# A fused attention and mixture-of-experts kernel: constants, weight casts and the interleaving of a batch's steps with the FFN are reordered

## The chip, the cores and the metric

The kernel runs on one core of a Trainium2 chip. The metric is the device time of one execution in microseconds (us). A comparison of two kernels is always made on one chip, in rounds that run both; the time of the kernel before differs between chips by up to 1.4% (medians from 247.9 to 251.3 us in this study), so ratios are compared across calls, and absolute times only within one. All runs quoted here are in what the record calls the fast state: none is over 1.5% above the fastest of its kernel in the same rounds.

The engines are named as the profile names them: PE is TensorE (matmuls), PEld its weight loads, DVE is VectorE, ACT is ScalarE, POOL is GpSimd, SP is SyncE.

## The reference

```python
# q, k, v: (batch 8, heads 8, seq 576, head_dim 64), fp32
def _attn_ref(q, k, v):
    q_s = exp(q - max over dims);  q_s /= sum over dims + 1e-9
    k_s = exp(k - max over seq);   k_s /= sum over seq + 1e-9
    kv = np.einsum('bhsd,bhse->bhde', k_s, v)
    return np.einsum('bhsd,bhde->bhse', q_s, kv)

# x: the 4608 tokens of 512 elements; 8 experts of 1024 hidden elements
def _moe_ref(x, modality_id, w_gate, modality_bias, w1, w2):
    logits = x @ w_gate + modality_bias[modality_id]
    e_idx = np.argmax(logits, axis=1)
    gate_w = softmax(logits)[token, e_idx]
    for e in range(E):
        mask = e_idx == e
        h = np.maximum(x[mask] @ w1[e], 0.0)
        out[mask] = gate_w[mask, None] * (h @ w2[e])
```

(Shortened: the two softmaxes and the token reshaping are written in one line each.)

## The kernel before

The kernel loads two experts: the one that each modality's bias row favours. (A loop at the end redoes tokens that chose another; it is not entered here.) It goes through the eight batches in order. For each, `prep` exponentiates k and q on ScalarE and casts v; `attend` multiplies k with v (`kv_ps`), scales the result into `kvbd`, turns q and kv (`tp_ps`, `kvT_ps`), and gets the logits (`g_ps`, `lg_ps`); `route` decides the expert of each token, counts places (`r_ps`), and moves the tokens, sorted, into `xs` (`xT_ps`). Each is a generator. `weave` runs a batch's steps and, at every `yield x`, adds `x * rate` to what is owed in FFN pieces of earlier batches. A piece is some 0.9 us of matmuls (0.86 us from the one at 75.81 us in batch 2 to what follows it); it keeps PE busy while the other engines work on the batch.

```python
def prep(b, v_eng):                      # six steps: k, k, v, v, q, q
    ...
            for nm in "kvq":
                ...                      # v: copy_on(v_eng, vb, st);  k, q: ACT Exp
                yield

def attend(b):
    for hp in range(2):
        for j in range(NJ):
            ...                          # kv_ps += ek.T @ vb
            if j == 4:
                yield 0.5
        if hp == 0:
            yield 0.5
    ...                                  # DVE: kinv, kvbd <- kv_ps
    yield 1.5
    ...
        for c0, nj in groups:            # ((0, 4), (4, 4), (8, 1))
            turn(c0, nj, 0)              # PE: tp_ps <- eq turned
            turn(c0, nj, 1)
            turned(c0, nj)               # et <- tp_ps, on ACT where c0 == 4, else DVE
            if nj > 1:
                yield 1.2 if c0 == 0 else 2
        kvT = kv_turned()                # PE: kvT_ps <- kvbd turned; ACT: kvT <- kvT_ps
    yield 2.6
    ...                                  # PE: g_ps <- kvT, wg_sb;  DVE: gx <- g_ps
    yield 2
    ...                                  # PE: lg_ps <- et, gx;     DVE: qi, lw
    yield 2.3

def route(b):
    ...                                  # DVE: lg, eqm, kk, isa, pos;  ACT: exp
    xps = [x_tile(b, 0)]                 # PE: x_ps, one of two buffers
    yield 1.6
    xps.append(x_tile(b, 1))
    yield 2.4
    ...                                  # PE: r_ps <- isa;  DVE: qi, aoff, pos, perm
    scale(0)                             # DVE: x_sb <- x_ps * qi
    scale(1)
    yield 4.2
    free[0] = nc.vector                  # y_ps is copied out by DVE from here on
    for t in range(NT):                  # five tiles
        ...                              # PE: xT_ps <- x_out[t], perm
        if t + 2 < NT:
            xps.append(x_tile(b, t + 2))
        ...                              # ACT: xs <- xT_ps, twice (an 'a' and a 'b' end)
        yield 1.4 if t < NT - 1 else 2
        if t + 2 < NT:
            scale(t + 2)
    free[0] = nc.scalar

def slots(b):
    ...                                  # DVE: slot, hi, lo, hhi, hlo;  POOL: hv <- hhi, vals

def places(b):
    id_ps = sp_ps.tile([P, 3, NSL], FP32, name="id_ps", tag="sp")   # pool of one buffer,
    ...                                  # PE: id_ps <- hlo, hv     # shared with g, lg, r
    ...                                  # DVE: lst, idb, ab, sel

def batch(b):
    side = chain(attend(b), route(b))
    for i, x in enumerate(side):
        if i == 3 and b > 2:
            slots(b - 1)
        if i == 7 and b > 2:
            places(b - 1)
        yield x

for b in range(2, B):
    weave(batch(b), (12 if b == 2 else 15.5) / 28.9, prep(b + 1, nc.gpsimd) if b + 1 < B else (), 4)
```

The start, in program order (cut to the calls):

```python
xs_w = [nc.gpsimd.memset(xs[:, kd, :].bitcast(FP32), 0.0) for kd in (2, 3)]
...                                      # plane 0: ACT, plane 1: DVE (below)
gating()         # DVE: the two experts; the bias parts; PE: bias spread over partitions
...              # SP: loads of weights and batches
xs_w.append(nc.vector.memset(xs[:, 1, :].bitcast(FP32), 0.0))
p0, p1 = prep(0, nc.vector), prep(1, nc.scalar)
steps(p0, 4)     # both halves of batch 0's k and v
...
places(0)        # in batch 1's route
mains(1)
cast_weights(1, 0, nc.gpsimd)            # W <- st, 128x2048, slot 1
cast_weights(1, 1, nc.gpsimd)
steps(r1, 1)
mains(2)
cast_weights(1, 2, nc.gpsimd)
cast_weights(1, 3, nc.gpsimd)
weave(r1, 0.8)
```

The softmax here doesn't subtract the row's maximum and nothing guards it: scores larger than these inputs give would overflow.

Of the kernel before, what the change touches and what calls it, by code (L numbers as in the profile page):

```python
# [11 lines left out]
FP32 = mybir.dt.float32  # L12
# [30 lines left out]
def kernel(  # L43
# [114 lines left out]
    ident = const.tile([P, P], BF16)  # L158
    make_identity(nc, ident)
# [4 lines left out]
    for i in range(2):  # L164
        nc.gpsimd.memset(vb_b[i][:, :, :, 128:130], 1.0)
        nc.gpsimd.memset(et_b[i][:, :, 576:640], 0.0)
        nc.vector.memset(kvbd_b[i], 0.0)
        nc.vector.memset(gx_b[i], 0.0)
        nc.vector.memset(gx_b[i][0:64, :, 16:17], 1.0)
        nc.vector.memset(gx_b[i][64:128, :, 17:18], 1.0)  # L170
    ones = const.tile([P, P], BF16)
# [46 lines left out]

    xs = persist.tile([P, KD, NSLOT], BF16)
    lst = persist.tile([P, 3, NSL], FP32)  # L220
    nc.gpsimd.memset(lst, 0.0)

    xs_w = [nc.gpsimd.memset(xs[:, kd, :].bitcast(FP32), 0.0) for kd in (2, 3)]
# [10 lines left out]
    modf = const.tile([P, B, NT], FP32)  # L234
    biasd = const.tile([P, E], FP32)
    nc.vector.memset(modf, 0.0)
    xs_w.append(nc.scalar.copy(out=xs[:, 0, :].bitcast(FP32), in_=view(modf, [[0, NSLOT // 2]])))

    def gating():
# [7 lines left out]
        key_1 = const.tile([1, 2], FP32, name="key_1")  # L247
# [11 lines left out]

        nb = 2 * E  # L260
        parts = const.tile([1, 4, nb], BF16, name="parts")
# [6 lines left out]
        nc.vector.tensor_copy(out=parts[:, 3, 0:2], in_=key_1)  # L268
        b_ps = sp_ps.tile([P, 2 * nb], FP32, name="b_ps", tag="sp")
# [21 lines left out]
    def biases():  # L291

        nc.scalar.copy(out=mbf, in_=view(mraw, [[2, NJ], [2 * NJ, 64]]))  # L293
        m_ps = sp_ps.tile([P, NT, B], BF16, name="m_ps", tag="sp")
        for t in range(NT):
            j0, nj = (2 * (t - 1), 2) if t else (NJ - 1, 1)
            nc.tensor.transpose(
                out=m_ps[0 : tsz[t], t, :], in_=view(mbf, [[1, 64 * nj]], 64 * j0), identity=ident[0:B, 0:B]
            )
        nc.vector.tensor_copy(out=view(modf, [[1, NT - 1], [NT, B]], 1), in_=m_ps[:, 1:NT, :])  # L300
        nc.vector.tensor_copy(out=modf[0:64, :, 0], in_=m_ps[0:64, 0, :])

        nc.vector.tensor_sub(out=biasd, in0=bias_b[:, 1, :], in1=bias_b[:, 0, :])
        nc.vector.tensor_tensor(
            out=bsel, in0=view(modf, [[1, B * NT], [0, E]]), in1=view(biasd, [[0, B * NT], [1, E]]), op=ALU.mult
        )

    def bias_of_tokens():
        nc.vector.tensor_tensor(
            out=bsel, in0=bsel, in1=view(bias_b, [[0, B * NT], [1, E]]), op=ALU.add  # L310
        )
# [26 lines left out]
    def cast_weights(s, part, eng):  # L338
        copy_on(eng, W[:, s, part * 2 * F : (part + 1) * 2 * F], wst.pop((s, part))[:, 0 : 2 * F])
# [36 lines left out]
    def attend(b):  # L376
# [5 lines left out]
        for hp in range(2):  # L382
            for j in range(NJ):
                for hg in range(2):
                    rows = slice(64 * hg, 64 * hg + 64)
                    nc.tensor.matmul(  # L386
                        out=kv[hg][:, 130 * hp : 130 * hp + 129],
                        lhsT=ek[rows, j, P * hp : P * hp + P],
                        rhs=vb[rows, j, hp, 0:129],
                        start=(j == 0),  # L390
                        stop=(j == NJ - 1),
                    )
                if j == 4:
                    yield 0.5
            if hp == 0:
                yield 0.5
# [16 lines left out]
        yield 1.5  # L413
# [38 lines left out]
        else:  # L452
            for c0, nj in groups:
                turn(c0, nj, 0)
                turn(c0, nj, 1)
                turned(c0, nj)
                if nj > 1:
                    yield 1.2 if c0 == 0 else 2
            kvT = kv_turned()
        yield 2.6  # L460
# [7 lines left out]
        yield 2  # L468
# [25 lines left out]
        yield 2.3  # L494
# [16 lines left out]
    lws, qis, ids, sorted_ = {}, {}, {}, []  # L511
# [19 lines left out]
    def route(b):  # L531
# [25 lines left out]
        yield 1.6  # L557
        xps.append(x_tile(b, 1))
        yield 2.4
# [32 lines left out]
        nc.vector.tensor_tensor(  # L592
# [11 lines left out]
        yield 4.2  # L604
        free[0] = nc.vector
        for t in range(NT):
# [18 lines left out]
            yield 1.4 if t < NT - 1 else 2  # L625
# [193 lines left out]
    def weave(side, rate, preps=(), first=0):  # L819
# [3 lines left out]
        for i, x in enumerate(side):  # L823
            if i >= first:
                next(preps, None)
            owed += x * rate
            while owed >= 1:
                mains(1)
                owed -= 1
# [12 lines left out]
    gating()  # L842
# [7 lines left out]
    xs_w.append(nc.vector.memset(xs[:, 1, :].bitcast(FP32), 0.0))  # L850

# [10 lines left out]
    p0, p1 = prep(0, nc.vector), prep(1, nc.scalar)  # L862
    steps(p0, 4)
    a0 = attend(0)
    steps(a0, 2)
    gate_weights()
    biases()
    steps(a0, 2)
# [46 lines left out]
    cast_weights(1, 0, nc.gpsimd)  # L915
    cast_weights(1, 1, nc.gpsimd)
    steps(r1, 1)
    mains(2)
    cast_weights(1, 2, nc.gpsimd)
    cast_weights(1, 3, nc.gpsimd)  # L920
    weave(r1, 0.8)
# [10 lines left out]
    def batch(b):  # L932
        side = chain(attend(b), route(b))
        for i, x in enumerate(side):
            if i == 3 and b > 2:
                slots(b - 1)
            if i == 7 and b > 2:
# [3 lines left out]
    for b in range(2, B):  # L941
        weave(batch(b), (12 if b == 2 else 15.5) / 28.9, prep(b + 1, nc.gpsimd) if b + 1 < B else (), 4)
# [147 lines left out]
```

## Time and profile before

| | before |
|---|---|
| median of three runs | 250.0 us (249.95 to 250.34) |
| span of the profiled run | 249.0 us |
| PE busy | 197.4 us, 79% |
| first kv matmul of batch 0 | 13.2 us |
| first FFN matmul | 38.9 us |
| last batch's tokens moved (last xT matmul) | 202.4 us |
| mean granted clock | 0.974 |

The prediction below shows the slices, the stretches and PE's waits, and why idle time of PE before 202 us is what counts. Two views are added here. The first is ScalarE's timeline in batch 5. Its columns are start, length, engine, line, operation, output from input, shapes, count.

```profile
135.91 1.02 ACT L351 COPY et<-tp_ps 128x1024 bf16<-128x1024 bf16 x1
136.81 1.18 ACT L369 ACTIVATE ek<-st 128x1152 bf16<-128x1152 f32 x1
...
138.35 0.60 ACT L440 COPY kvT<-kvT_ps 128x512 bf16<-128x512 bf16 x1
```

Between the copy of the turned q (`et`) and that of the turned kv (`kvT`), for which PE waits, ScalarE does 1.18 us of the next batch's `prep`. The prediction did not read this line, and it is needed below.

The second is PE's timeline in batch 2, with a group of four matmuls at about half the clock (1.80 us instead of 1.03; the granted clock was 0.54 from 71.8 to 73.6 us); in brackets the wait ahead of an instruction and who ended it. The prediction reads this spell as a loss of its own, and b_places will be held against it.

```profile
70.34 0.25 PE L463 MATMUL g_ps<-wg_sb,kvT 128*128 128x8 bf16 x4 [1.70 <-ACT kvT L440]
...
71.83 1.80 PE L737 MATMUL y_ps<-W,hT 128*128 128x512 bf16 x4
```

### The profile page before, as it was taken

The numbers are of one execution on the slowest core, as the hardware profiler recorded it, in microseconds if no ns is written. First come the engines' busy times: TensorE is split into PE (matmuls) and PEld (weight loads), VectorE is DVE, ScalarE is ACT, GpSimd is POOL, SyncE is SP. The second block draws the span as 40 slices with busy tenths as digits, with TensorE's granted clock in tenths as the row PEclk, the third lists the DMA queues.
The fourth block names the chain that finished last, engine by engine and source line by source line (L and its number), as shares of the span: only waits on it lengthen the run. The fifth ranks groups of instructions, "written<-read, shape, count | busy, mean of one in ns | idle before, by whom it ended". The sixth has DMA issues, their size and how long they took to land. (4 is left out here: it accounts for less than half of the span.)

```text
span 249.0 us, 5372 instructions
## 1 busy us (share of the span) xinstructions
PE 197.4 (79%) x2016; PEld 137.5 (55%) x2016; DVE 155.9 (63%) x507; ACT 148.0 (59%) x233; POOL 81.8 (33%) x90
## 2 busy tenths in 40 slices
PE   0078569899878889797989888986998789999960
PEld 0067447576734567465746654664557546758620
DVE  6868988775448477845875795789565775520120
ACT  4937785669765686567865757664833473526300
POOL 8400616185703242217021701360133016041340
PEclk9999997999979999999999999999999999999995
DMA  6999999999999519622962101120112003021220
GB/s 221 370 391 400 391 406 387 391 394 371 336 405 389 230 50 364 235 95 53 371 235 87 45 0 42 45 84 3 42 43 87 1 21 117 36 100 68 77 86 10
DMA packets 18937, 46.55 MB, mean 187 GB/s; under 512 B 1229, under 2 KB 1229, under 8 KB 18910
## 3 DMA queue, kind: packets, MB, share of 16 engines
q1 hardware_dynamic: 15920, 36.70, 40.3%
q0 software_dynamic: 2960, 9.44, 9.8%
q8 instruction: 16, 0.26, 0.4%
q14 instruction: 11, 0.09, 0.1%
q10 hardware_dynamic: 30, 0.05, 0.1%
HBM read 36.75 MB, written 9.70 MB: 187 GB/s over the span
## 5 line engine op out<-in xcount | busy, mean ns | idle before, releaser
L750 POOL DMA_INDIRECT out_dram<-y_sb,ix x37 | 36.6, 989 | 115.0 <-DVE y_sb L351 36.3
L737 PE MATMUL y_ps<-W,hT 128*128 128x512 bf16 x288 | 71.7, 385 | 0.1
L719 PE MATMUL h_ps<-xs,W 128*128 128x256 bf16 x576 | 70.6, 274 | 0.1
L719 PEld LDWEIGHTS <-W 128*128 128x128 bf16 x576 | 54.5, 98 | 7.1 <-issue 0.4
L730 ACT ACTIVATE hT<-h_ps 128x512 bf16<-128x512 f32 x69 | 40.6, 597 | 28.0 <-PE h_ps L719 26.2
L622 ACT CAST xs<-xT_ps 128x512 f32 (+2 forms) x80 | 39.5, 557 | 12.6 <-PE xT_ps L610 11.0
L737 PEld LDWEIGHTS <-hT 128*128 128x128 bf16 x296 | 26.8, 98 | 25.1 <-issue 1.8
L351 DVE COPY y_sb<-y_ps 128x512 f32<-128x512 f32 x17 | 11.8, 692 | 35.1 <-PE y_ps L737 32.4
L351 ACT COPY y_sb<-y_ps 128x512 f32<-128x512 f32 x20 | 11.7, 585 | 31.7 <-PE y_ps L737 30.1
L573 DVE TENSOR_TENSOR x_sb<-x_ps,qi 128x512 bf16<-128x512 f32 (+1 forms) x40 | 26.2, 681 | 1.9 <-PE x_ps L502 1.2
L610 PE MATMUL xT_ps<-perm,x_sb 128*128 128x128 bf16 (+1 forms) x160 | 14.8, 214 | 13.1 <-DVE x_sb L573 10.1
L610 PEld LDWEIGHTS <-x_sb 128*128 128x128 bf16 (+1 forms) x160 | 10.3, 97 | 22.8 <-DVE x_sb L573 18.6
L652 POOL TENSOR_TENSOR hv<-hhi,vals 128x570 bf16<-128x570 bf16 x8 | 12.5, 1568 | 27.0 <-DVE hhi L648 27.0
L369 ACT ACTIVATE eq<-st 128x1152 bf16<-128x1152 f32 x16 | 18.4, 1156 | 0.2 <-DMA st<-in_q_dram 0.2
L369 ACT ACTIVATE ek<-st 128x1152 bf16<-128x1152 f32 x16 | 18.5, 1166 | 0.0
L386 PE MATMUL kv_ps<-vb,ek 64*128 64x129 bf16 x288 | 12.1, 228 | 6.5 <-DVE vb L351 3.9
L351 POOL CAST W<-st 128x2048 bf16<-128x2048 f32 x6 | 11.4, 1924 | 17.3 <-DMA st<-in_moe_w_dram 17.3
L502 PE MATMUL x_ps<-kvbd,et 128*128 128x128 bf16 (+1 forms) x160 | 16.3, 229 | 0.0
L386 PEld LDWEIGHTS <-ek 64*128 64x128 bf16 x288 | 9.5, 99 | 12.0 <-ACT mbf L293 5.8
L422 PE MATMUL tp_ps<-ident,eq 128*128 128x128 bf16 x144 | 12.6, 231 | 1.8 <-ACT et L351 1.8
L351 POOL CAST vb<-st 128x1152 bf16<-128x1152 f32 x12 | 13.5, 1151 | 0.0
L422 PEld LDWEIGHTS <-eq 128*128 128x128 bf16 x144 | 10.5, 104 | 5.2 <-issue 3.0
(151 smaller groups left out, 227.2 us busy)
## 6 DMA issues: line engine op xcount, KB each, us to landing
st<-in_k_dram SPq DMA_DIRECT2D x8, 1152.0 KB, 5.7
st<-in_moe_w_dram SPq DMA_DIRECT2D x8, 1024.0 KB, 11.9
st<-in_v_dram SPq DMA_DIRECT2D x7, 1152.0 KB, 8.1
st<-in_q_dram SPq DMA_DIRECT2D x6, 1152.0 KB
st<-in_q_dram SPq DMA_DIRECT2D x4, 576.0 KB, 13.1
st<-in_v_dram SPq DMA_DIRECT2D x2, 576.0 KB, 7.5
out_dram<-y_sb,ix POOLq DMA_INDIRECT x37, 2.8
W<-in_moe_modality_id_dram ACTq DMA_DIRECT2D x1, 36.0 KB
```

The lines of the kernel that those rows point to most:

```text
L351: return (nc.scalar.copy if eng is nc.scalar else eng.tensor_copy)(out=out, in_=in_)
L369: nc.scalar.activation(out=view((eks if nm == "k" else eqs)[b], [[Dh, 2], [HG * Dh, NJ], [1, Dh]], 2 * g * Dh), in_=src[:, 2 * g : 2 * g + ...
L386: nc.tensor.matmul(out=kv[hg][:, 130 * hp : 130 * hp + 129], lhsT=ek[rows, j, P * hp : P * hp + P], rhs=vb[rows, j, hp, 0:129], start=(j = ...
L422: nc.tensor.transpose(out=view(tp[c0], [[2 * nj * 64, 2], [1, 64]], hp * nj * 64 + jj * 64), in_=eq[:, c0 + jj, P * hp : P * hp + P], iden ...
L502: nc.tensor.matmul(out=view(x_ps, [[2 * Dh, 2], [1, Dh]], (4 * (p_ % 2) + p_ // 2) * Dh, (0, T)), lhsT=et[:, p_, tcol[t] : tcol[t] + T], r ...
L573: nc.vector.tensor_tensor(out=view(x_out[t], [[2 * Dh, HG], [Dh, 2], [1, Dh]], 0, (0, T)), in0=view(xps[t], [[2 * Dh, HG], [Dh, 2], [1, Dh ...
L610: nc.tensor.matmul(out=xT_ps[:, kd, 0:T], lhsT=x_out[t][0:T, kd * P : (kd + 1) * P], rhs=perm[0:T, t, 0:T], start=True, stop=True,)
L622: w = nc.scalar.copy(out=window(a + off, b, T, off > 0), in_=xT_ps[:, :, 0:T])
L719: nc.tensor.matmul(out=h_ps[:, f * w : (f + 1) * w], lhsT=w1(kd * F + (f0 + f) * P, P), rhs=x_in[:, kd, :], start=(kd == 0), stop=(kd == K ...
L730: nc.scalar.activation(out=h_out, in_=h_in, func=ACT.Relu)
L737: nc.tensor.matmul(out=y_ps, lhsT=hT[:, kf, t * P : (t + 1) * P], rhs=w2(kf * D, D), start=(kf == 0), stop=(kf == KF - 1),)
L750: store = nc.gpsimd.indirect_dma_start(out=out, out_offset=bass.IndirectOffsetOnAxis(ap=ix[:, t : t + 1], axis=0), in_=y_sb, in_offset=Non ...
```

## The change

The intent is in five parts. (1) **Start**: GpSimd clears three planes of `xs` ahead of its constants, VectorE none; VectorE casts the first half of v before the expert choice, and the bias parts and their spread come later. (2) **Casts of slot 1**: all four wait until batch 1's `perm` is built. (3) **kv turned ahead**: after the second turned group instead of the third. (4) **Places in the next batch's kv**: `slots` at step 0 instead of 3, `places` at step 4 instead of 7. (5) **Spread**: the weights of the yields are changed, so that pieces lie where latency is, and the steps of `prep` for the next batch move from steps 4 to 9 to steps 2, 3, 4, 5, 7 and 8.

```diff
+    xs = persist.tile([P, KD, NSLOT], BF16)
+    modf = const.tile([P, B, NT], FP32)
+    nc.vector.memset(modf, 0.0)
+    xs_w = [nc.gpsimd.memset(xs[:, kd, :].bitcast(FP32), 0.0) for kd in range(1, KD)]
+    xs_w.append(nc.scalar.copy(out=xs[:, 0, :].bitcast(FP32), in_=view(modf, [[0, NSLOT // 2]])))
+    ident = const.tile([P, P], BF16)
+    make_identity(nc, ident)                       # moved here from above
...
-    xs_w = [nc.gpsimd.memset(xs[:, kd, :].bitcast(FP32), 0.0) for kd in (2, 3)]
...
-    def gating():
+    def experts():                                 # gating, split in experts,
...                                                 # bias_parts and spread
@@ attend
                 if j == 4:
-                    yield 0.5
+                    yield 0.2
             if hp == 0:
-                yield 0.5
+                yield 0.2
...
-        yield 1.5
+        yield 0.8
...
                 turned(c0, nj)
+                if c0 == 4:
+                    kvT = kv_turned()
                 if nj > 1:
-                    yield 1.2 if c0 == 0 else 2
-            kvT = kv_turned()
-        yield 2.6
+                    yield 0.8
+        yield 1
...                                                 # after g
-        yield 2
+        yield 1.2
...                                                 # after the logits
-        yield 2.3
+        yield 1.4
@@ route
-        yield 1.6
+        yield 0.8
         xps.append(x_tile(b, 1))
-        yield 2.4
+        yield 1.3
...                                                 # after scale(1)
-        yield 4.2
+        yield 3.3
...                                                 # after each tile
-            yield 1.4 if t < NT - 1 else 2
+            yield 0.7 if t < NT - 1 else 1
@@ weave
-            if i >= first:
+            if i in at:
                 next(preps, None)
@@ start
-    gating()
+    p0, p1 = prep(0, nc.vector), prep(1, nc.scalar)
+    for _ in range(3):
+        next(p0)
+    experts()
...
-    xs_w.append(nc.vector.memset(xs[:, 1, :].bitcast(FP32), 0.0))
-    p0, p1 = prep(0, nc.vector), prep(1, nc.scalar)
-    steps(p0, 4)
+    steps(p0, 1)
+    bias_parts()
...
@@ batch 1
-    cast_weights(1, 0, nc.gpsimd)
-    cast_weights(1, 1, nc.gpsimd)
     steps(r1, 1)
+    after(cast_weights(1, 0, nc.gpsimd), [perm_of[1]], ...)
+    for part in range(1, 4):
+        cast_weights(1, part, nc.gpsimd)
     mains(2)
-    cast_weights(1, 2, nc.gpsimd)
-    cast_weights(1, 3, nc.gpsimd)
-    weave(r1, 0.8)
+    weave(r1, 2)
@@ batch
-            if i == 3 and b > 2:
+            if i == 0 and b > 2:
                 slots(b - 1)
-            if i == 7 and b > 2:
+            if i == 4 and b > 2:
                 places(b - 1)
@@ loop
-        weave(batch(b), (12 if b == 2 else 15.5) / 28.9, prep(...), 4)
+        weave(batch(b), (12 if b == 2 else 15.5) / 15.4, prep(...), (2, 3, 4, 5, 7, 8))
```

More of the change, by code (lines that the diff above doesn't have):

```diff
@@ L157 @@
     nc.gpsimd.iota(iota_i, pattern=[[1, E]], base=0, channel_multiplier=0)
-    ident = const.tile([P, P], BF16)
-    make_identity(nc, ident)
     kvbd_b = [persist.tile([P, NP, P], BF16, name=f"kvbd{i}") for i in range(2)]
@@ L217 @@
     wgb = ybuf.tile([P, D], FP32, name="y_sb").bitcast(BF16)
-    xs = persist.tile([P, KD, NSLOT], BF16)
     lst = persist.tile([P, 3, NSL], FP32)
     nc.gpsimd.memset(lst, 0.0)
-    xs_w = [nc.gpsimd.memset(xs[:, kd, :].bitcast(FP32), 0.0) for kd in (2, 3)]
     aoff_i = persist.tile([1, B * NT], I32)
@@ L233 @@
     bsel = const.tile([P, B * NT, E], FP32)
-    modf = const.tile([P, B, NT], FP32)
     biasd = const.tile([P, E], FP32)
-    nc.vector.memset(modf, 0.0)
-    xs_w.append(nc.scalar.copy(out=xs[:, 0, :].bitcast(FP32), in_=view(modf, [[0, NSLOT // 2]])))
-    def gating():
+    key_1 = const.tile([1, 2], FP32)
+    parts = const.tile([1, 4, 2 * E], BF16)
+    def experts():
         bmx = const.tile([1, 2], FP32, name="bmx")
@@ L246, in gating @@
         nc.vector.tensor_tensor(out=beq, in0=beq, in1=view(wrow, [[0, 2], [1, E]], 0, (0, 1)), op=ALU.mult)
-        key_1 = const.tile([1, 2], FP32, name="key_1")
         nc.vector.reduce_max(out=key_1, in_=beq, axis=AX.X)
@@ L258, in gating, with bias_parts @@
         )
+    def bias_parts():
         nb = 2 * E
-        parts = const.tile([1, 4, nb], BF16, name="parts")
         left = const.tile([1, nb], FP32, name="left")
@@ L268, in gating, with spread @@
         nc.vector.tensor_copy(out=parts[:, 3, 0:2], in_=key_1)
+    def spread():
+        nb = 2 * E
         b_ps = sp_ps.tile([P, 2 * nb], FP32, name="b_ps", tag="sp")
@@ L301, in biases, with bias_of_tokens @@
         nc.vector.tensor_copy(out=modf[0:64, :, 0], in_=m_ps[0:64, 0, :])
+    def bias_of_tokens():
         nc.vector.tensor_sub(out=biasd, in0=bias_b[:, 1, :], in1=bias_b[:, 0, :])
@@ L306, in biases @@
         )
-    def bias_of_tokens():
         nc.vector.tensor_tensor(
@@ L338, in cast_weights @@
     def cast_weights(s, part, eng):
-        copy_on(eng, W[:, s, part * 2 * F : (part + 1) * 2 * F], wst.pop((s, part))[:, 0 : 2 * F])
+        return copy_on(eng, W[:, s, part * 2 * F : (part + 1) * 2 * F], wst.pop((s, part))[:, 0 : 2 * F])
     def after(ins, befores, why):
@@ L509, in x_tile @@
         return x_ps
-    lws, qis, ids, sorted_ = {}, {}, {}, []
+    lws, qis, ids, sorted_, perm_of = {}, {}, {}, [], {}
     FIRST = [next(x for x in passes if x[0] == ph and x[1] == 0) for ph in range(NPH)]
@@ L591, in route @@
         perm = sb.tile([P, NT, P], BF16, name="perm")
-        nc.vector.tensor_tensor(
+        perm_of[b] = nc.vector.tensor_tensor(
             out=perm, in0=view(iota_row, [[0, NT], [1, P]]), in1=view(pos, [[1, NT], [0, P]]), op=ALU.is_equal
@@ L817, in mains, with weave @@
                 now[0] += 1
-    def weave(side, rate, preps=(), first=0):
+    def weave(side, rate, preps=(), at=()):
         owed = 0.0
@@ L866 @@
     gate_weights()
+    steps(a0, 2)
+    spread()
     biases()
-    steps(a0, 2)
     steps(p0, 2)
@@ L914 @@
     mains(1)
-    cast_weights(1, 0, nc.gpsimd)
-    cast_weights(1, 1, nc.gpsimd)
     steps(r1, 1)
+    after(cast_weights(1, 0, nc.gpsimd), [perm_of[1]], "GpSimd and VectorE share a port")
+    for part in range(1, 4):
+        cast_weights(1, part, nc.gpsimd)
     mains(2)
-    cast_weights(1, 2, nc.gpsimd)
-    cast_weights(1, 3, nc.gpsimd)
-    weave(r1, 0.8)
+    weave(r1, 2)
     slots(1)
@@ L941 @@
     for b in range(2, B):
-        weave(batch(b), (12 if b == 2 else 15.5) / 28.9, prep(b + 1, nc.gpsimd) if b + 1 < B else (), 4)
+        weave(
+            batch(b),
+            (12 if b == 2 else 15.5) / 15.4,
+            prep(b + 1, nc.gpsimd) if b + 1 < B else (),
+            (2, 3, 4, 5, 7, 8),
+        )
     big = persist.tile([1, 2], I32)
```

## The prediction

> **What bounds the kernel now.** I read the page's slices first, then the stretches table cut at the start of each batch's kv matmuls, then PE's waits, then the timeline where the waits lie. The slices:
>
> ```profile
> PE   0078569899878889797989888986998789999960
> PEclk9999997999979999999999999999999999999995
> ```
>
> PE is idle for two slices of 6.2 us, patchy until 39 us, mostly busy after that. The stretches (us, then busy us and instructions of each engine, granted clock, DMA share, GB/s):
>
> ```profile
> 0.00:13.10 13.10, 0.66 (x4) 0.40 (x4) 10.40 (x35) 9.63 (x7) 7.87 (x27) 1.00 0.87 300
> 22.20:38.90 16.70, 11.22 (x177) 9.52 (x176) 14.69 (x50) 12.77 (x19) 6.70 (x4) 0.97 1.04 398
> ...
> 62.50:85.34 22.84, 18.25 (x189) 11.46 (x189) 12.38 (x40) 15.35 (x26) 7.61 (x8) 0.93 0.98 368
> 85.34:108.74 23.40, 20.00 (x222) 14.20 (x222) 16.17 (x54) 15.61 (x27) 6.74 (x7) 1.00 0.53 186
> ...
> 131.50:155.44 23.94, 20.33 (x223) 14.20 (x223) 17.36 (x53) 15.64 (x27) 6.79 (x7) 1.00 0.12 45
> 155.44:179.80 24.36, 20.32 (x223) 14.12 (x223) 18.21 (x52) 15.93 (x28) 7.73 (x7) 1.00 0.09 34
> ...
> 203.20:241.00 37.80, 36.62 (x261) 23.54 (x258) 12.37 (x53) 15.64 (x27) 13.23 (x13) 1.00 0.20 76
> ```
>
> From 203 us PE runs the leftover FFN pieces almost without a gap. A PE gap closed earlier therefore shortens the end by as much. The gaps before that are the reserve: 22.84 - 18.25 = 4.6 us in batch 2, then 3.4, 2.75, 3.6, 4.0 and 3.8 us in batches 3 to 7 (the rows not shown are worked the same way), 22 us in all. Before 39 us it is a latency chain on VectorE: 14.69 of 16.7 us busy in the third stretch. DMA is at 0.98 or more until 85 us, but PE's waits name no DMA. PE's waits (total us, times, longest):
>
> ```profile
> PE xT_ps L610 <- DVE x_sb L573: 10.1, 12, 1.9
> PE g_ps L463 <- ACT kvT L440: 5.4, 6, 1.7
> PE kv_ps L386 <- DVE vb L351: 3.9, 1, 3.9
> PE id_ps L669 <- DVE gx L467: 2.8, 5, 0.8
> ```
>
> Each batch waits for the scaled tile x_sb, for the turned kv (kvT) and for the place counts, which share a PSUM buffer with gx. The start waits for the first value cast. VectorE's timeline shows what holds it (start, length):
>
> ```profile
> 4.69 2.33 DVE L266 CAST parts<-left 1x16 bf16<-1x16 f32 x1
> 10.33 2.08 DVE L850 MEMSET xs<- 128x2432 f32 x1 [0.45 <-issue]
> 12.33 1.36 DVE L351 CAST vb<-st 128x1152 bf16<-128x1152 f32 x2
> 25.57 1.75 DVE L567 TENSOR_TENSOR qi<-qi,gsum 128x40 f32<-128x40 f32 x1
> 39.85 1.71 DVE L537 TENSOR_TENSOR lg<-lg,bsel 128x40 f32<-128x40 f32 x1
> 164.51 2.68 DVE L674 SCALAR_TENSOR_TENSOR idb<-lst 128x38 f32<-128x38 f32 x1
> ```
>
> Sixteen elements take 2.33 us beside GpSimd's xs memset (from 4.88), qi 1.75 beside a weight cast (25.37 to 27.26), lg's bias add 1.71 beside weight casts (37.78 to 41.51). These are stalls, not work.
>
> [...] x_sb, sourced in PSUM, took its usual 0.68 us under the casts at 50 us. [...] here idb sat through two value casts back to back (164.88 to 167.13). [...] The trace shows halved matmuls (4 in 1.80 us, not 1.03) at 71.8 us, after a mere 1.70 us wait for kvT.
>
> **The change part by part.**
>
> (1) Start. VectorE loses the 2.08 us memset and casts v before the bias parts; GpSimd clears three planes, 3 x 2.1 us from about 2 us, done near 8.3. v's half loads take 7.5 us from issue at 1.4 to 2 us, so about 8.4 and 9.9: the first cast ends near 9.2 instead of 13.0. The expert choice (9 small operations, 1.65 us) comes next and puts eid_i from 4.4 to about 11, harmless: the weights are issued at 11.05 into a queue full until about 20 us. The second kv half needs the gate weights' copy (ScalarE, 11.0), so kv ends near 12.9 instead of 16.4. Most of these 3.5 us go again: the bias spread and mask turning now sit behind kvbd (near 15.4 before turning starts), q's second half is exponentiated only at 14.64, and two 0.49 us bias operations come before qi. So the logits are about 0.8 us earlier (qi 20.25 instead of 21.05). If that beats the weight cast's start at 25.37, which DMA sets, the 1.55 us excess of qi goes too, but perm follows at about 25.45 and may be caught instead. Gain between 0.5 and 2.3, taken as 1.2 us. In batch 1 kvT earlier gives nothing: gx there waits for VectorE's slot chain until 36.8.
>
> (2) Weight casts of slot 1 behind perm of batch 1. The 1.5 us excess of the lg add leaves VectorE; PE only waited 0.7 us there. All four casts (4 x 1.9 = 7.5 us) now start near 46 us and end near 53, so slot 1's first FFN waits a few tenths at most. Gain 0.5, with a risk under the rivals.
>
> (3) kv turned ahead. Two FFN pieces (2 x 0.87 us) lie between kvT's matmuls and g instead of one, and ScalarE copies kvT straight after et. The 0.66 us wait of a batch, 1.7 in batch 2, goes; in batch 2 the half-clock spell goes too: 0.7 + 0.8 us on the two slow 4-matmul groups.
>
> (4) Slots before kvbd, places after the first turned group. The 0.48 us wait and the places' chain (up to 2.7 us with its stall) leave the stretch between g and qi. But id now needs hv early: slots take 1.35 us to hhi, then hv on GpSimd about 1.6. In about half of the batches VectorE reaches slots only after a y_sb copy, 0.8 us into kv; then hv ends near 3.8 us and PE, there at 2.9, waits about 0.9. Average 0.5.
>
> (5) Pieces by latency. Same number (15 in batch 3 in both orders). From r to the first xT there are now four instead of two or three: 3.5 us against the 3.0 needed, so its 0.6 to 1.1 us goes. From logits to r three instead of four: 3.2 us of PE work against qi-to-isa 3.47 + 0.2, a new wait of 0.5, where batches 6 and 7 had 1.26 and 0.49. In the xT stretch three pieces instead of four: 4.4 us of PE work while ScalarE's ten copies need 0.65 + 8 x 0.51 = 4.7 and gaps. So kv waits about 1.2 us for its two banks, where xT and kv waited 0.5 to 1.2 in all.
>
> Sum per batch 3 to 7: after 1.2 + 0.5 + 0.5 + 0.3 unforeseen = 2.5 us idle against 3.5, 5 x 1.0 = 5.0 us. Batch 2: g 1.7, xT 2.1 and clock 1.5 go; only two pieces before r add 1.3, ScalarE's bank wait 1.0, the rest uncertain; net 2.0. Total 1.2 + 0.5 + 2.0 + 5.0 = 8.7 us. Against this the risk in the first rival, weighed at 1.2. 250.0 - 7.5 = 242.5.
>
> **Rivals.**
>
> (A) [...] The index row ix (two SBUF-sourced columns on VectorE) now comes while four casts run back to back. Against hv it took 1.10 us instead of 0.15. If it gets in between two casts it loses 1 to 2 us, hidden by a piece. If it sits through all of them, as idb through two, x_sb of the last tiles comes up to 6 us late and PE loses about 4. A cast slipped between two memsets at 7.02 us, which speaks against it; one chance in four. Time then 246.
>
> (B) ScalarE becomes the local bound. It works 15.6 of 23.5 us in a batch; its ten copies are now crowded behind fewer pieces, with both ek activations right after. Then kv waits 1.5 to 2 us per batch, the closed gaps return there, and 246 to 248 results.
>
> (C) Everything closes: hv always ready, r not waited for, perm ahead of the cast. Then idle falls to about 1.2 us per batch, and 236 to 238 results.
>
> (D) DMA binds the early part. Its share of 1.0 speaks for it, the lack of DMA waits on PE against it; only the weight cast's start at 25.37 hangs on it. It would cap (1) at 0.5.
>
> **Range and chances.** The middle is 242.5. A and B together put the upper end at 247.5, C the lower at 237.5. 2% is 245.0: only one of A or B in full crosses it, so faster 0.68, within 2% 0.29, slower 0.03, as nothing is added to PE and its order stays full.
>
> **What will show it.** PE's waits: g on kvT gone; xT on x_sb down from 10.1 to under 4 us; id on gx replaced by id on hv in some batches; a new wait of r on isa and a larger one of kv on xs. The stretches: batches 3 to 7 near 22.5 us. The first kv matmul near 9 to 10 us, the first FFN matmul near 37.7 instead of 38.9; the lg add at 0.20 us. Wrong would be: batch stretches unchanged with kv waiting on xs over 1.5 us, or an ix of several us in batch 1.

## The result

On the same chip the kernel before took 250.17 us (median of 4 runs, 249.95 to 252.57) and the changed one 237.92 us (median of 4, 237.31 to 239.31). The ratio is 0.9497, with a 95% interval of 0.9426 to 0.9569: faster by 5.0%. A ratio is the mean time of one kernel's fast runs over the mean of the other's fast runs in the same rounds, so it is not quite the ratio of the two medians. In the traces the span went from 249.0 to 236.1 us, at granted clocks of 0.974 and 0.973, so the mean clock explains nothing of it; where the low clock lies did change (below).

Where the 12.9 us of span came from, by the times of landmarks in the two traces:

| stretch | before | after | gain |
|---|---|---|---|
| to the first FFN matmul | 38.89 | 36.68 | 2.2 |
| to batch 2's first kv matmul (batch 1's route) | 23.61 | 23.64 | 0.0 |
| batch 2 | 22.84 | 20.00 | 2.8 |
| batches 3 to 7, to the last xT matmul | 117.07 | 109.78 | 7.3 |
| tail | 46.6 | 46.0 | 0.6 |

Each column is one trace, and a stretch of one trace is not exact: in b_loop, a_cast_early and a_experts_first (below), whose batches 2 to 7 have the same code as the changed kernel's, batches 3 to 7 took 108.3 us. The number of FFN pieces in each stretch from batch 2 on is the same before and after (counted in a_ref, the second trace of the changed kernel).

The slices of the changed kernel (busy tenths of PE, then the granted clock, in 40 slices of 5.9 us):

```profile
PE   0267869899898789979998997989898989999950
PEclk9999797999999999999999999999999999999995
```

PE has something to do from the second slice on. The kernel before had the clock at 7 in the seventh slice (the end of the start) and in the twelfth (batch 2); here the seventh still shows it, the fifth does too, also within the start, and batch 2 keeps its full clock. These spells differ between traces of one code: a_preps_late, which has the same start, shows none (mean clock 0.989) and reaches batch 2's first kv matmul at 58.5 us, against 60.3 here and in a_ref (0.973 and 0.974) and 61.0 in a_places_late (0.975), which show both.

The stretches of the changed kernel, cut at the same landmarks (columns as in the prediction: the stretch and its length, then busy us and instructions of PE, its weight loads, VectorE, ScalarE and GpSimd, granted clock, DMA share, GB/s):

```profile
22.20:36.68 14.48, 10.61 (x164) 9.19 (x162) 12.25 (x47) 12.44 (x18) 5.43 (x3) 0.85 1.03 399
...
60.32:80.32 20.00, 16.72 (x187) 11.10 (x189) 12.32 (x40) 15.18 (x26) 7.60 (x8) 1.00 1.05 399
80.32:102.91 22.59, 19.68 (x221) 14.16 (x223) 16.89 (x61) 16.02 (x28) 7.70 (x7) 1.00 0.71 252
...
123.55:145.72 22.17, 19.54 (x219) 14.15 (x222) 16.41 (x60) 16.28 (x29) 7.76 (x7) 1.00 0.10 39
145.72:167.72 22.00, 20.14 (x220) 13.98 (x223) 16.10 (x45) 15.61 (x27) 6.77 (x6) 1.00 0.13 48
```

VectorE's busy time in the first of these fell from 14.69 to 12.25 us. Of that, 1.55 us is the stall of `qi`, which went; the two stretches do not hold quite the same work (50 and 47 instructions). In batch 2 the clock is 1.00 where it was 0.93, and PE idles 3.3 us instead of 4.6. In batches 3, 5 and 6 it idles 2.9, 2.6 and 1.9 us instead of 3.4, 3.6 and 4.0; in batch 4, whose row is left out, 0.8 instead of 2.75. The figures of after are even a little too high, since this trace lacks 19 of the 288 second-layer matmuls that were recorded before.

PE's waits of the changed kernel (line waited at, who released it, total us, times, longest):

```profile
...
PE xT_ps L616 <- DVE x_sb L579: 5.1, 7, 1.6
PE r_ps L567 <- DVE isa L555: 4.5, 7, 1.2
PE lg_ps L478 <- DVE gx L473: 2.5, 3, 1.5
...
PE kv_ps L391 <- ACT xs L628: 1.7, 5, 0.6
PE id_ps L675 <- POOL hv L658: 1.6, 3, 0.8
PE xT_ps L616 <- ACT xs L628: 1.4, 2, 1.2
```

The wait of `g_ps` on `kvT` (5.4 us before) is in the list no more, nor is that of `id_ps` on `gx` (2.8 us). `x_sb` holds PE for 5.1 us instead of 10.1. In their place stand a wait of the counts `r_ps` on the expert mask `isa`, 4.5 us, and small ones on GpSimd's `hv` and ScalarE's `xs`. The wait of the logits `lg_ps` on `gx` grew from 1.1 to 2.5 us; 1.5 of that is in batch 1.

VectorE's timeline where the stalls had been:

```profile
9.05 0.77 DVE L356 CAST vb<-st 128x1152 bf16<-128x1152 f32 x1 [0.63 <-DMA st<-in_v_dram]
...
24.55 0.20 DVE L573 TENSOR_TENSOR qi<-qi,gsum 128x40 f32<-128x40 f32 x1
25.24 0.83 DVE L598 TENSOR_TENSOR perm<-iota_row,pos 128x640 bf16<-128x640 bf16 x1
...
45.79 0.86 DVE L689 TENSOR_SCALAR ix<-sel 128x2 int32<-128x2 f32 x1
```

And GpSimd's, the one cast that matters to `perm`, with the wait ahead of it in brackets:

```profile
25.96 1.89 POOL L356 CAST W<-st 128x2048 bf16<-128x2048 f32 x1 [13.61 <-DMA st<-in_moe_w_dram]
```

The first v cast waits for its load alone and ends at 9.8 instead of 13.0. `qi` takes 0.20 us where it had taken 1.75, and `perm`, at its usual 0.83 us, comes ahead of the weight cast rather than being caught by it. That cast starts at 25.96 instead of 25.37 us; the profile names its load as what ended the wait, and whether `perm` held it for a moment can't be told from it. `ix` under the four casts of slot 1 lost 0.7 us (0.86 instead of 0.15), and no more.

ScalarE's timeline in batch 5, to be held against the one of before:

```profile
129.25 1.02 ACT L356 COPY et<-tp_ps 128x1024 bf16<-128x1024 bf16 x1
130.16 0.60 ACT L445 COPY kvT<-kvT_ps 128x512 bf16<-128x512 bf16 x1
```

`kvT` follows `et` at once. Two parts of the change do this together: kv is turned earlier, and the `ek` of the next batch is somewhere else.

### The profile page after: what moved, and what is told of

It is laid out like the page before. It is cut to its first block, busy times and chain, and to the rows that moved or that the text cites. A ratio compares the mean times of both kernels' runs of the same rounds, so it can differ in the third digit from the quotient of the medians.

```text
span 236.1 us, 5347 instructions
## 1 busy us (share of the span) xinstructions
PE 193.8 (82%) x1997; PEld 137.9 (58%) x2016; DVE 150.6 (64%) x503; ACT 148.9 (63%) x236; POOL 84.8 (36%) x91
## 5 line engine op out<-in xcount | busy, mean ns | idle before, releaser
L743 PE MATMUL y_ps<-W,hT 128*128 128x512 bf16 x269 | 67.4, 379 | 1.5 <-ACT hT L736 0.5
L356 ACT COPY y_sb<-y_ps 128x512 f32<-128x512 f32 x22 | 12.9, 586 | 29.0 <-PE y_ps L743 27.7
L356 DVE COPY y_sb<-y_ps 128x512 f32<-128x512 f32 x15 | 10.4, 692 | 32.7 <-PE y_ps L743 28.2
L374 ACT ACTIVATE ek<-st 128x1152 bf16<-128x1152 f32 x16 | 17.9, 1165 | 0.0
L508 PEld LDWEIGHTS <-et 128*128 128x128 bf16 (+1 forms) x160 | 10.9, 104 | 2.8 <-issue 2.1
```

Of the source, the lines that this page charges most:

```text
L356: return (nc.scalar.copy if eng is nc.scalar else eng.tensor_copy)(out=out, in_=in_)
L374: nc.scalar.activation(out=view((eks if nm == "k" else eqs)[b], [[Dh, 2], [HG * Dh, NJ], [1, Dh]], 2 * g * Dh), in_=src[:, 2 * g : 2 * g + ...
L508: nc.tensor.matmul(out=view(x_ps, [[2 * Dh, 2], [1, Dh]], (4 * (p_ % 2) + p_ // 2) * Dh, (0, T)), lhsT=et[:, p_, tcol[t] : tcol[t] + T], r ...
L743: nc.tensor.matmul(out=y_ps, lhsT=hT[:, kf, t * P : (t + 1) * P], rhs=w2(kf * D, D), start=(kf == 0), stop=(kf == KF - 1),)
```

## The experiments

Twelve kernels ran, all with correct results and all in the fast state. The expectations were written on a base of 250 us. The first four ran on one chip (kernel before: 249.24 us), the next four on a second (247.9), the last four on a third (251.33). Names beginning with b_ are the kernel before with one part added; with a_, the changed kernel with one part undone or altered. "Of before" is the ratio to the kernel before in the same rounds, with its 95% interval. By the study's own verdict, which asks for 2%, b_start is "same" and b_places "unclear", though neither interval holds 1; all others are "faster".

| run | median us | of before |
|---|---|---|
| the changed kernel at first | 237.92 | 0.9497 (0.9426 to 0.9569) |
| b_start | 245.31 | 0.9852 (0.9804 to 0.9899) |
| b_loop | 238.01 | 0.9579 (0.9517 to 0.9641) |
| a_spread_old | 237.24 | 0.9519 (0.9473 to 0.9564) |
| a_kv_late | 236.64 | 0.9502 (0.9457 to 0.9547) |
| a_places_late | 241.12 | 0.9722 (0.9679 to 0.9764) |
| a_preps_late | 236.61 | 0.9555 (0.9497 to 0.9612) |
| a_cast_early | 235.90 | 0.9522 (0.9482 to 0.9563) |
| a_experts_first | 236.19 | 0.9517 (0.9455 to 0.958) |
| a_ref (the changed kernel again) | 237.63 | 0.9468 (0.944 to 0.9496) |
| a_kv_preps_late | 243.53 | 0.9702 (0.9668 to 0.9737) |
| b_places | 245.99 | 0.9826 (0.9789 to 0.9863) |
| a_scale_first | 232.63 | 0.9267 (0.924 to 0.9294) |

### b_start and b_loop: do the start and the rest add up?

b_start is the kernel before with part (1) alone. b_loop has everything but part (1).

```diff
 # b_start, against the changed kernel: the loop as it was
-            if i == 0 and b > 2:                 # slots; places likewise
+            if i == 3 and b > 2:
-            (2, 3, 4, 5, 7, 8),
+            (4, 5, 6, 7, 8, 9),
 # and: old yields, kv_turned() after the groups, casts of slot 1 as before
 # b_loop: the kernel before with these in their new form, its start untouched
```

> The kernel before with the changed start alone (clearing ahead of GpSimd's constants, gating behind the first value cast); loop and weight casts as before. Theory: the start and the loop close PE gaps in separate stretches, so the 2.2 us by which the first FFN matmul came earlier (38.9 to 36.7) stay to the end: 247.6 to 248.4 us. Rival: the start is bound by the transfers, and what it gains is given back before batch 2: 249.5 to 250.3 us.

> The kernel before with everything but the changed start. Theory: separate stretches add, so 250.1 less the 9.9 to 10.7 us that the stretches from 39 us on became shorter: 239.5 to 240.5 us. Rival: the two parts need each other (the loop's gains hang on loads that the earlier start frees): 242 us or more.

The start alone is worth 3.7 us (1.5%, 1.0 to 2.0), the rest alone 10.5 us (4.2%). The product of the two ratios, 0.9437, is the ratio of the whole kernel within the intervals, so the two parts add and neither hides the other. The start gave more than the 2.2 us by which the first FFN matmul comes earlier in the trace. In the trace of b_start the first FFN matmul is 2.5 us earlier than before, batch 2's kv 2.9 us, and the rest comes later, partly because a stalled `idb` near 140 us took 0.72 us instead of 1.56, and PE's wait at `r_ps` in batch 7 went. The author takes it that GpSimd's casts met VectorE's place chain at another moment; this was not put to a test. Taken the other way, as what the changed kernel gains on b_loop, the start is worth 0.8 to 1.1 points (2.1 to 2.8 us), with an uncertainty that holds 3.7 as well. And the 2.2 us come from a trace with two spells of low clock in the start: by the 58.5 us of a_preps_late at batch 2 the same start gains 4.0 us.

### a_spread_old: the yields as before

```diff
-        yield 1.2            # and every other yield of attend and route,
+        yield 2              # all back to the old weights
-    weave(r1, 2)
+    weave(r1, 0.8)
-            (12 if b == 2 else 15.5) / 15.4,
+            (12 if b == 2 else 15.5) / 28.9,
```

> The changed kernel with the old weights for spreading the FFN pieces (sum 28.9, batch 1 at 0.8). Theory: the spread carries about half of the loop's gain, as it puts four pieces instead of two or three behind r; the wait of the first xT for x_sb comes back with 0.6 to 1.1 us per batch and r's wait goes: 241 to 243 us. Rival: the order of kv and places carries nearly all: under 239.3 us.

The expectation missed: the kernel is as fast as the changed one within the uncertainty. Only batch 2 is plainly different, 21.88 instead of 20.00 us. PE's timeline there:

```profile
73.98 0.29 PE L616 MATMUL xT_ps<-perm,x_sb 64*128 64x64 bf16 x4 [2.00 <-DVE x_sb L579]
...
76.03 1.91 PE L743 MATMUL y_ps<-W,hT 128*128 128x512 bf16 x4
```

A wait of 2.00 us is followed by four matmuls in 1.91 us where four of this form take 1.03 at the full clock. In the changed kernel the waits of batch 2 are 1.15 us at the most and the clock stays at 1.00. But the wait alone does not bring the spell. b_places (below) has the batch 2 of the kernel before, unchanged. Its clock and PE's timeline there:

```profile
PEclk9999999999999999999999999999999999999995
```

```profile
70.34 0.26 PE L463 MATMUL g_ps<-wg_sb,kvT 128*128 128x8 bf16 x4 [1.69 <-ACT kvT L440]
...
71.83 1.02 PE L737 MATMUL y_ps<-W,hT 128*128 128x512 bf16 x4
...
78.63 0.29 PE L610 MATMUL xT_ps<-perm,x_sb 64*128 64x64 bf16 x4 [2.00 <-DVE x_sb L573]
...
79.08 1.03 PE L737 MATMUL y_ps<-W,hT 128*128 128x512 bf16 x4
```

The same waits, and no spell; b_start shows the same. Nor does the spell cost what it lasts: batch 2 took 22.84 us with it and 22.57 and 22.56 without, since PE then waits 2.00 us for `x_sb` instead of 1.14. So by these traces 0.3 us of batch 2's gain is the clock, and the rest is the change.

The new weights of the yields are worth something in batch 2, and nothing measurable over the whole. In batches 3 to 7 the trace of a_spread_old is even the shorter one (107.4 us, against 108.3 in a_cast_early and 109.8 in the changed kernel), at a tail 0.7 us longer. There the new weights take from the wait of `xT_ps` on `x_sb` and add to that at `r_ps` (7.3 and 0.9 us here, 5.1 and 4.5 in the changed kernel, 3.5 and 3.0 in a_cast_early).

### a_kv_late, a_preps_late and a_kv_preps_late: two cures for one wait

```diff
 # a_kv_late
-                if c0 == 4:
-                    kvT = kv_turned()
                 if nj > 1:
                     yield 0.8
+            kvT = kv_turned()
         yield 1
 # a_preps_late
-            (2, 3, 4, 5, 7, 8),
+            (4, 5, 6, 7, 8, 9),
 # a_kv_preps_late: both
```

> The changed kernel with kv turned after the last q group again. Theory: g waits for kvT again, 0.7 us in batches 3 to 7 and up to 1.7 us in batch 2, possibly with the half-clock spell: 241 to 243 us. Rival: the later r wait shrinks by as much, as VectorE's chain and not g sets the batch: under 239 us.

> The changed kernel with the next batch's exponentials and value casts at steps 4 to 9 in a row, as before, instead of 2, 3, 4, 5, 7, 8. Theory: the two value casts on GpSimd fall on VectorE's chain between logits and r [...]; r's wait rises from 4.5 us in all to 7 or more: 239.5 to 242 us. Rival: the place of the casts is free, as the places no longer lie in that chain: 237.3 to 238.6 us.

> The changed kernel with both kv turned late and the next batch's exponentials late. Each alone cost almost nothing. Theory: both close the same wait: before, an ek exponential of 1.18 us stood between et and kvT on ScalarE, and either moving it or turning kv ahead is enough; with both undone g waits for kvT by about 0.7 us again in each batch (3.5 to 5 us in all on PE) and the time is 3 to 5 us above the reference. Rival: they are independent and both worthless: less than 1.5 us above the reference.

Turning kv late again cost nothing measurable (the expectation of 241 to 243 us missed), and the old `prep` steps alone cost nothing outside the uncertainty (0.6 points to the first run of the changed kernel, the intervals overlapping; 0.9 to its second, the intervals just touching). The expectation for it, 239.5 to 242 us by a wait at `r_ps` of 7 us or more, missed too: that wait was 3.8 us. Its four runs fall in two pairs, 235.5 and 235.7 us at a clock of 0.989, 237.5 twice at 0.974, so a small cost can hide in it: in its trace batches 2 to 7 are 1.3 us longer than in a_cast_early. The theory formed from this was that either is enough to let ScalarE copy `kvT` without an `ek` in front. Both undone together confirm it: 243.53 us, 5.9 us more than a_ref in the same rounds, even somewhat more than expected. PE's wait is back, at more than its size in the kernel before:

```profile
PE g_ps L468 <- ACT kvT L445: 6.5, 6, 1.2
```

In that trace `ek` takes 1.18 us again between `et` (133.44) and `kvT` (135.89). In a_kv_late the wait came once only, with 1.1 us, in batch 1; in a_preps_late not at all. That it is larger than before in batches 3 to 6 (1.06 to 1.09 us instead of 0.66) goes with the new place of the places: b_places alone shows the same 1.06 to 1.09.

### a_places_late and b_places: the places alone

```diff
 # a_places_late, against the changed kernel; b_places is the reverse, on the kernel before
-            if i == 0 and b > 2:
+            if i == 3 and b > 2:
                 slots(b - 1)
-            if i == 4 and b > 2:
+            if i == 7 and b > 2:
                 places(b - 1)
```

> The changed kernel with slots and places at their old steps (slots behind kvbd, places behind g). Theory: id waits for gx again (0.5 us a batch), and the places' chain [...] lies between logits and r again, where now only three pieces cover it, so r waits 1 to 2.5 us more: 241 to 245 us. Rival: the 0.4 to 0.8 us waits on hv that the new place brought go away and balance it: 237 to 239 us.

> The kernel before with slots and places moved to their new steps and nothing else. Theory: the place of this chain is the largest single part (undoing it cost 5 to 6 us): 4 to 6.5 us below the kernel before, ratio 0.974 to 0.984, with id no longer waiting for gx. Rival: it needs the spread and the earlier casts to pay, as hv would be late and kvbd delayed: less than 2.5 us below.

This is the largest single part: without it the ratio is 0.9722 instead of 0.9468 to 0.9497, some 2.0 to 2.5% or 5 to 6 us (the interval of that difference is about 1.4 to 3.1 points); and alone on the kernel before it gives 1.7%, 4.4 us at its mean. Both are as expected. PE's waits in a_places_late, then VectorE's and PE's timelines in two of its batches, show what the old place of this work does:

```profile
PE r_ps L567 <- DVE isa L555: 6.1, 7, 1.4
...
PE id_ps L675 <- DVE gx L473: 2.9, 5, 1.0
```

```profile
133.83 1.82 DVE L680 SCALAR_TENSOR_TENSOR idb<-lst 128x38 f32<-128x38 f32 x1
```

```profile
163.10 0.18 PE L567 MATMUL r_ps<-isa,tri 128*128 128x5 bf16 x1 [1.38 <-DVE isa L555]
```

`idb` works on 38 columns and takes 0.20 us when nothing is in its way (as in batch 5 of the changed kernel). In a_places_late it takes 1.77, 1.82 and 1.94 us in three batches (4 to 6), put down to GpSimd's value casts (the author's estimate, from the like stalls beside them in the kernel before, 2.68 us, and in the changed one, below), and it stands between `gx` and `qi`, so the logits, `isa` and `r_ps` come later by as much. PE waits 1.22 to 1.38 us at `r_ps` in each of those batches, and 0.5 to 1.0 us for `gx` at `id_ps`. These three batches are 1.3 to 1.7 us longer than in the changed kernel, while batches 3 and 7, where nothing is caught, are up to 0.5 us shorter. In the changed kernel the chain is still caught in two batches, even for longer: `idb` 2.44 us from 107.26 us, and `sel`, the last of the chain, 2.81 us from 150.5 us (a_ref has both with the same lengths), each under two value casts (107.40 to 109.64 and 151.00 to 153.24 us in the changed kernel). But there only a copy of turned q and `gx` stand behind it, with g's matmuls and a piece still to come: PE then waits 0.26 us at `r_ps` in the first of these batches, and 0.30 at `lg_ps` and 0.52 at `r_ps` in the second. VectorE's and PE's timelines in the first, in the changed kernel:

```profile
107.26 2.44 DVE L680 SCALAR_TENSOR_TENSOR idb<-lst 128x38 f32<-128x38 f32 x1
```

```profile
114.83 0.18 PE L567 MATMUL r_ps<-isa,tri 128*128 128x5 bf16 x1 [0.26 <-DVE isa L555]
```

The stalled operations sum to 5.3 us in the changed kernel and 5.5 in a_places_late. So the change has not removed these stalls; it has moved them to where PE hardly waits for them.

### a_cast_early: slot 1's casts as before

```diff
-    steps(r1, 1)
-    after(cast_weights(1, 0, nc.gpsimd), [perm_of[1]], ...)
-    for part in range(1, 4):
-        cast_weights(1, part, nc.gpsimd)
+    cast_weights(1, 0, nc.gpsimd)
+    cast_weights(1, 1, nc.gpsimd)
+    steps(r1, 1)
     mains(2)
+    cast_weights(1, 2, nc.gpsimd)
+    cast_weights(1, 3, nc.gpsimd)
```

> The changed kernel with slot 1's weight casts where they were, two before and two after batch 1's second route step. Theory: they stall lg's bias add for 1.5 us again, but PE has FFN pieces there and waits at most 0.7 us more: 237.6 to 238.8 us. Rival: r and the first xT of batch 1 move with VectorE's chain: 239.2 us or more.

The ratio is that of the changed kernel within the uncertainty. The stalls do come back on VectorE (lg's bias add 0.87 us, `isa` 1.50 us), and PE's waits in batch 1 stay the same, 0.73 and 0.29 us. The gating is worth nothing that was measured here: batch 1 waits for something else.

### a_experts_first: the expert choice ahead of the first v cast

```diff
-    for _ in range(3):
+    for _ in range(2):
         next(p0)
     experts()
 ...
-    steps(p0, 1)
+    steps(p0, 2)
     bias_parts()
```

> The changed kernel with the choice of the experts ahead of both value casts. Theory: the small operations wait for GpSimd's three memsets up to 8.2 us (wrow did, 5.69 us), so the first cast ends 1.5 to 2 us later, but the second kv half waits for the gate weights' copy (11.0) and the chain to the logits for q: 237.5 to 239 us, the first FFN at most 1 us later. Rival: all of the start's 2.2 us hang on this order: 239.8 us or more.

The first kv matmul moves from 9.96 to 10.79 us, but `qi` of batch 0 is at 20.13 instead of 20.02 and the first FFN matmul at 36.66 instead of 36.68 us. In the order of the start it is not this swap that counts.

### a_ref and a_scale_first: what the changed kernel still waits for

The largest wait left was `xT_ps` on `x_sb`. The scaling of tile t+2 is issued after the yield, that is behind the FFN piece, so on VectorE it stands behind that piece's copy of `y_sb`, which itself waits for the piece's last matmul. a_scale_first issues it before.

```diff
             if t + 2 < NT:
                 xps.append(x_tile(b, t + 2))
+                scale(t + 2)
 ...
             yield 0.7 if t < NT - 1 else 1
-            if t + 2 < NT:
-                scale(t + 2)
```

> The changed kernel again, as the reference for the runs of this call and for the size of what chance moves: ratio 0.948 to 0.956 to the kernel before, 235.5 to 238 us.

> The changed kernel with each x_sb scaled ahead of the FFN pieces of its step, so that no y_sb copy stands before it on VectorE. Theory: xT's waits for x_sb (5.1 us in the changed profile, up to 1.57 us where a y_sb copy came first) fall under 2 us, but ScalarE's ten copies bind next: 1 to 2.5 us below the reference. Rival: ScalarE's copies are already the limit there and the wait only moves to kv: within 0.7 us of the reference.

VectorE's timeline in a_ref, in batch 5:

```profile
143.16 0.69 DVE L356 COPY y_sb<-y_ps 128x512 f32<-128x512 f32 x1 [1.33 <-PE y_ps L743]
143.77 0.68 DVE L579 TENSOR_TENSOR x_sb<-x_ps,qi 128x512 bf16<-128x512 f32 x1
```

VectorE's timeline in a_scale_first, at the same place:

```profile
138.78 0.69 DVE L579 TENSOR_TENSOR x_sb<-x_ps,qi 128x512 bf16<-128x512 f32 x1 [0.47 <-PE x_ps L508]
139.65 0.69 DVE L356 COPY y_sb<-y_ps 128x512 f32<-128x512 f32 x1 [0.17 <-PE y_ps L742]
```

And PE's waits in a_scale_first:

```profile
PE kv_ps L391 <- ACT xs L629: 3.5, 5, 0.8
...
PE xT_ps L616 <- DVE x_sb L579: 1.2, 3, 0.7
```

In a_ref VectorE idles 1.33 us for the end of the piece while the tile to be scaled is ready behind it. With the order swapped it scales first. PE's wait for `x_sb` falls from 5.1 to 1.2 us, that of `xT_ps` on `xs` from 1.4 to nothing, that of `id_ps` on `hv` from 1.6 to 0.4, while that of `kv_ps` on ScalarE's `xs` grows from 1.7 to 3.5: 4.7 us less in sum. The time is 232.63 us against 237.63 in the same rounds, 5.0 us less, twice and more of what was expected. This is the fastest kernel of the study, 7.3% below the kernel before. What it waits for next is ScalarE's copies of moved tokens.

## Why the prediction was right, and where its sizes were off

The direction and the range were right: 237.92 us lies in 237.5 to 247.5, close to the low end and 4.6 us below the middle. The mechanism held too: PE has no gaps of note once the batches are through (the tail is 46.0 us after 46.6), the start gained more than the 0.5 us that rival D allowed, PE's gaps in the batches were the reserve, and closing them shortened the end. The terms, one by one:

- **Start: 1.2 us predicted, 2.2 us in the landmarks, 3.7 us (2.5 to 4.9) alone.** The working named the open point, whether `qi` and `perm` come ahead of the weight cast. Both did: `qi` at 24.55 and `perm` at 25.24, while the cast came at 25.96, 0.6 us later than before. The step that failed is the cautious choice near the lower end of 0.5 to 2.3. The 2.2 us are the low end of what the traces show: 4.0 by the trace of a_preps_late, whose start has no spell of low clock. The rest was read as a shift of later stalls of VectorE, and was not tested.
- **Casts of slot 1: 0.5 us predicted, none measured.** The stretch of batch 1 is 23.61 and 23.64 us, and undoing the gating cost nothing. The risk weighed against it, rival A, did not happen either: `ix` lost 0.7 us, between the first and the second cast.
- **kv ahead: the wait on `kvT` went, as predicted.** But the working put the whole of it down to the earlier turning. It overlooked that the `prep` steps move too, which by itself takes `ek` from ahead of `kvT`. Only undoing both brings the wait back, at 5.9 us.
- **The half-clock spell of batch 2: 1.5 us predicted, 0.3 measured.** With the same batch 2 and no spell, b_places and b_start were 0.3 us faster there. The spell had stood largely where PE would otherwise have waited for `x_sb`.
- **Places: counted as neutral, measured at 4 to 6 us.** This is the mis-sized term. The prediction set the 0.48 us wait of `id_ps` that goes against a new one on `hv` of 0.5, and said that the chain of up to 2.7 us leaves the stretch between g and qi, but gave it no value of its own. The wait on `hv` was 0.77, 0, 0.40, 0 and 0.40 us, 0.31 on average. What a chain caught between gx and qi costs at `r_ps`, 1.22 to 1.38 us of waiting in each of three batches of a_places_late, was not in the sum: the prediction had that wait depend on the number of pieces only.
- **Spread: the new wait at `r_ps` was 0.25 to 1.02, 0.46 on average, against 0.5 predicted.** The wait of kv for ScalarE's banks was 0.2 to 0.6 against 1.2 predicted, too high. The wait for `x_sb` was said to go; 5.1 us of it stayed in the trace of the changed kernel (3.5 and 2.6 in a_cast_early and a_experts_first), because a copy of `y_sb` stood ahead of the scaling on VectorE. The last two errors lie in opposite directions, so that the total came near is in part luck.
- **Sums.** Batch 2 gave 2.8 against 2.0; batches 3 to 7 gave 7.3 against 5.0. The 1.2 us taken off for rival A were not needed (one chance in four of the 4 us named there would be 1.0).
- **Rivals.** B (ScalarE as the bound) did not come, except as the next limit in a_scale_first. C, "everything closes", named the time of the result, 236 to 238, but not its way: 2.9, 0.8, 2.6 and 1.9 us of idle time are left in batches 3 to 6, 2.1 on average and not 1.2. The start gave more than the middle estimate instead. C's own terms do not give its range either: 1.2 us of idle time in five batches instead of 3.5, with the other terms as they stand, is 15.2 us off, near 235.
- **Readings.** The DMA share was 0.98 or more only from 13 us on; the first stretch shows 0.87. And not every operation of VectorE was stalled beside a memset of GpSimd: in the kernel before, `parts<-left,parts`, with two SBUF inputs, took 0.16 us at 7.05 us, under memsets from 4.88 to 9.09. Nothing above rests on it.

Of what was said to show it: g on kvT gone, held; xT on x_sb under 4 us, missed with 5.1, though held in two later traces with the same batches; id on hv in some batches, held; batches near 22.5 us, held, at 20.6 to 22.6; the first FFN matmul near 37.7, earlier at 36.7.

Open are what the start is worth exactly, between 2.1 and 4 us, and how much of that is the clock at the start; and the value of the new spread and of the gating, which is below what these rounds resolve.

## What to carry to other kernels

Ask of a small operation on a shared engine what stands behind it in that engine's order, and put it where nobody on the critical path stands behind: moving the places, and scaling a tile before the piece rather than after it, gave 4 to 6 us and 5 us without one instruction less. Before a wait is put down to one part of a change, list every part that shortens it, since two cures for one wait each look worthless when undone alone. What a stalled operation costs is read at the next wait of the bounding engine: `idb`, 0.20 us when free, was followed by a PE wait of 0.26 us at `r_ps` when it took 2.44 us in the changed kernel, and by one of 1.38 us when it took 1.94 us in a_places_late.

## What the traces leave open about the stalls and the clock

- A VectorE operation beside GpSimd's work did not always get in when the first GpSimd instruction ended: in the changed kernel `wrow` sat through three xs memsets in a row (5.69 us for 8 columns, from 2.49, beside memsets from 1.76 to 8.01; it took 0.11 us in the kernel before), and in the kernel before `idb` sat through two casts (2.68 us), while in the changed kernel `ix` got in between the first and second of four casts (0.86 us), and in the kernel before a cast of 16 elements between two memsets (2.33 us). Which of the two happens could not be told beforehand from these traces.
- Waits of 1.70 us (kernel before) and 2.00 us (a_spread_old) were followed, within some 2 us, by a group of four matmuls at about half the clock (1.80 and 1.91 us instead of 1.03). The same waits in the batch 2 of b_start and b_places (1.69 and 2.00 us) were not, nor was one of 1.57 us in the changed kernel. So the length of one wait does not decide, and what does is not shown here.
